# First batch of a windowed attention: casting loads on 128 rows, 64x64 matmuls per head, a new opening order

## The chip, the cores and the metric

The kernel runs on one core of a Trainium2 chip. The metric is device time in microseconds. The kernel before takes 319.98 us (median of 3 runs, 319.39 to 320.38).

## The reference

Attention with a symmetric window of 32, then a two-layer product with a leaky ReLU:

```python
# q, k, v: [8 batches, 8 heads, 576 tokens, 64]
scores = q @ k.T / 8, masked to |i - j| <= 32
attn   = softmax(scores)              # exp, row sums, division
x      = (attn @ v), heads side by side      # [4608, 512]
out    = leaky_relu(x @ w_in, 0.01) @ w_out  # w_in 512x2048, w_out 2048x512
```

## The kernel before

All matmuls run on bf16. Heads are taken in pairs: two heads of 64 columns fill 128 partitions. A batch has four pairs (`NPAIR`), and a batch's 576 tokens are worked in two halves of 288 (`HALF`), so that one attention step `i` is a batch, a half and a pair; batch 0 has steps 0 to 7, with half 0 in steps 0 to 3.

A step goes through four engines. `score(i)` multiplies keys and queries in five matmuls, one for each block of 64 keys that the window touches; ScalarE takes the exponential of both sets of 288 columns at once (`e`), and GpSimd multiplies it by the window's mask (`prob`, L282). `sums(i)` adds up the weights with a matmul by `ones_bd`, which is 1 in two diagonal blocks, and VectorE takes the reciprocal (L309). `product(i)` multiplies the weights with the values in five matmuls, and `scaled(i)` (L334) multiplies that by the reciprocal into `xT`, whose slice for pair `p` is the p-th of four chunks that `x @ w_in` sums over. To keep the two heads apart in matmuls over 128 rows, keys and values are stored as block diagonals, `kbd` and `vbd`, of 128x128 blocks with zeros off the diagonal; there are two buffers of each, which alternate by batch. They are cleared once, and only the diagonal blocks are written after that.

Queries and keys reach the kernel in one of two ways. In batches 0 and 1 (`b < BY_DMA`) they are loaded as 32-bit numbers on 96 rows (`load_qk`, L79), cast on VectorE or GpSimd (`cast_qk`, L197), transposed on TensorE (`transposes`, L225) and copied out of PSUM by ScalarE (L233, L239), after which `place_keys` copies the keys into `kbd` (L258). From batch 2 on, a transposing DMA does it. Values are loaded in two halves of 64 rows (`load_v`, L91) and cast into `vbd` (`cast_v`, L203 and L205). All these loads are issued by the SP queue. The weights `w_in` and `w_out` are cast by their DMAs, which GpSimd issues (L448, L452), in four quarters each.

The second part takes half by half (`g` = 0 to 15): 16 tiles `f` of hidden columns, each with four matmuls of 288 columns (`h_mms`, L348) and a leaky ReLU on ScalarE (`h_out`, L355), and for each 128 tokens one output tile of 16 matmuls (`o_tile`, L390).

The order of instructions is written out by hand (`manual_schedule`): an engine takes its instructions in the order in which the code records them and waits at each for its operands. The opening, from `cast_qk(0, 0, ...)` to the first tiles of half 1, is a list of such calls, with `keep_busy` matmuls between them that compute nothing of use; steps 4 to 7 are recorded between tiles of half 0 (`second_half`). From half 1 on, a plan of tiles with due times (`plan`, `due`, `spend`) records the attention steps of later batches between the tiles.

Of the kernel before, what the change touches and what calls it, by code (L numbers as in the profile page):

```python
# [9 lines left out]
FP32 = mybir.dt.float32  # L10
# [6 lines left out]
def kernel(  # L17
# [49 lines left out]

    def load_qk(b, p, behind=None):

        for into, src, name in ((qf, q, "qf"), (kf, k, "kf")):
            t = fload.tile([96, 2, RUN * D], FP32, name=f"{name}{p}")
# [13 lines left out]
    def load_v(b, p):  # L87

        t = fload.tile([128, NB, D], FP32, name=f"vf{p}")
        for a in range(2):  # L90
            nc.sync.dma_start(  # L91
                out=t[64 * a:64 * a + 64],
                in_=v[b, 2 * p + a].rearrange("(c p) d -> p c d", p=64),
            )
        vf[b, p] = t

    load_qk(0, 0)
    load_qk(0, 1)
    load_v(0, 0)
    load_qk(0, 2)  # L100
    load_qk(0, 3)
    for p in range(1, NPAIR):
        load_v(0, p)


    ident_f = const.tile([128, 128], FP32)
    make_identity(nc, ident_f)
    ident = const.tile([128, 128], BF16)
    nc.vector.tensor_copy(out=ident, in_=ident_f)

    ones_bd = const.tile([128, 128], BF16)
    nc.vector.memset(ones_bd, 0.0)
    nc.vector.memset(ones_bd[0:64, 0:64], 1.0)
    nc.vector.memset(ones_bd[64:128, 64:128], 1.0)


    qb = const.tile([96, NPAIR, RUN, 2, D], BF16)
    kb = const.tile([96, NPAIR, RUN, 2, D], BF16)

# [3 lines left out]
    nc.vector.memset(zero, 0.0)  # L123

    def clear(t, p):
        flat = t[:, p].rearrange("p n j -> p (n j)")
        nc.scalar.activation(
            out=flat, in_=zero.to_broadcast([128, NB * 128]), func=AF.Copy,
        )

    mask = [const.tile([128, 2, 2, EVEN], BF16, name=f"mask{i}") for i in range(2)]
    nc.vector.memset(mask[0][:, 1, :, 0:16], 0.0)
    nc.vector.memset(mask[1][:, 1, :, 128:EVEN], 0.0)
    nc.vector.memset(kbd[0], 0.0)
    clear(vbd[0], 0)
    clear(vbd[0], 1)
    clear(vbd[0], 2)


# [6 lines left out]
    win = const.tile([128, 2, 3, 64], BF16)  # L146
    nc.gpsimd.memset(win, 1.0)
    for lo in (0, 64):
# [3 lines left out]
            base=0, channel_multiplier=-1, pattern=[[1, 2], [0, 3], [2, 64]],  # L152
# [179 lines left out]
    def scaled(i):  # L332
        _, x, r = probs.pop(i)
        nc.vector.tensor_mul(place(i), x, r)  # L334
# [312 lines left out]
```

## Time and profile before

| | us |
|---|---|
| median of 3 runs | 319.98 (319.39 to 320.38) |
| span of the profiled execution | 318.5 |
| median less span | 1.5 |
| PE busy | 303.2 (95%) |
| VectorE (DVE) busy | 218.2 (69%) |
| GpSimd (POOL) busy | 191.6 (60%) |
| ScalarE (ACT) busy | 182.6 (57%) |
| PE busy, 0 to 5 us | 0.00 |
| PE busy, 5 to 10 us | 2.56 |
| PE busy, 10 to 15 us | 3.40 |
| PE busy, 20 to 25 us | 3.91 |

A profiled execution shows the span from the first to the last instruction; the measured time holds a little more. Busy time of an engine is the time in which one of its instructions runs; PEld is the loading of weights into the array, which runs beside the matmuls. Idle time costs something only where it lies on the chain of work that ends last. DMA queue q1 holds what SP issues and q0 what GpSimd issues; all of it runs on the same 16 DMA engines.

### The profile page before, as it was taken

The page shows a single profiled execution, that of the slowest core. Times are in us where ns is not written, and L with a number is a line of the kernel's source. Part 1 is how long each engine was busy: PE and PEld are TensorE (multiplying, and loading weights), DVE is VectorE, ACT ScalarE, POOL GpSimd, SP SyncE. Part 2 cuts the span into 40 slices and gives each one's busy share as a digit, 9 for nine tenths or more (in the row PEclk, how much of TensorE's full clock was granted, in tenths as well). Part 3 has the DMA queues.
Part 4 walks back from the last instruction along what each step waited for, and adds up shares of the span by engine and source line. Part 5 has one row for each costly group of instructions (what it writes and reads, how often), then busy time and mean ns, then how long its engine had stood idle before and what let it go on. Part 6 is the DMA issues. An engine that isn't in the chain of part 4 may idle for free.

```text
span 318.5 us, 6474 instructions
## 1 busy us (share of the span) xinstructions
PE 303.2 (95%) x2449; PEld 204.3 (64%) x2449; DVE 218.2 (69%) x259; ACT 182.6 (57%) x393; POOL 191.6 (60%) x251
## 2 busy tenths in 40 slices
PE   2679998999999999999999999999999999999996
PEld 1467774585765858576765858576665858576653
DVE  5678955869655997688755997688745988565100
ACT  7577698474652828374652828375552837464531
POOL 7798963974546866686546866586637866330000
PEclk9999999999999999999999999999999999999999
DMA  8999999997999995399735995399733430000101
GB/s 179 211 186 218 267 250 203 250 206 181 216 242 196 231 206 150 82 251 203 155 76 127 238 227 136 75 223 232 162 76 104 109 70 33 35 35 2 66 31 71
DMA packets 108400, 49.46 MB, mean 155 GB/s; under 512 B 68816, under 2 KB 103888, under 8 KB 108368
## 3 DMA queue, kind: packets, MB, share of 16 engines
q1 hardware_dynamic: 104144, 44.84, 66.8%
q0 software_dynamic: 4224, 4.19, 8.0%
q8 instruction: 19, 0.31, 0.4%
q14 instruction: 13, 0.11, 0.1%
HBM read 36.70 MB, written 9.44 MB: 145 GB/s over the span
## 4 chain that ended last, share of the span: by engine, by line
PE 89%; DMA 3%; DVE 2%; SPq 1%; POOL 1%; ACT 1%; issue 1%; DVEq 0%; ACTq 0%
PE mm L348 39%; PE mm L390 38%; PE x L320 5%; PE ps L275 4%; DMA kf<-in_k_dram 3%; PE s L301 2%; DVE r L309 2%; SPq L79 1%; POOL w_in_bf L448 1%; DVE xT L334 1%; PE tp L225 1%; PE s L304 1%; ACT vbd L203 0%; SPq L91 0%; POOL prob L282 0%
## 5 line engine op out<-in xcount | busy, mean ns | idle before, releaser
L309 DVE RECIPROCAL r<-s 128x288 f32<-128x288 f32 x64 | 125.2, 1956 | 56.5 <-PE s L301 53.3
L282 POOL TENSOR_TENSOR prob<-e,mask 128x576 bf16<-128x576 bf16 x64 | 81.5, 1274 | 87.8 <-ACT e L280 41.1
L348 PE MATMUL mm<-xT,w_in_bf 128*128 128x288 bf16 x1024 | 134.0, 286 | 0.3
L390 PE MATMUL mm<-w_out_bf,gT 128*128 128x512 bf16 (+2 forms) x592 | 130.4, 373 | 0.2 <-DMA w_out_bf<-in_moe_w_out_dram 0.2
L355 ACT ACTIVATE gT<-mm 128x288 bf16<-128x288 f32 x256 | 101.4, 412 | 24.8 <-PE mm L348 8.5
L348 PEld LDWEIGHTS <-w_in_bf 128*128 128x128 bf16 x1024 | 98.4, 98 | 24.8 <-issue 0.6
L390 PEld LDWEIGHTS <-gT 128*128 128x128 bf16 x592 | 56.3, 98 | 59.6 <-issue 0.3
L395 ACT ACTIVATE o_sb<-mm 128x512 f32<-128x512 f32 (+2 forms) x37 | 21.7, 586 | 92.0 <-PE mm L390 92.0
L280 ACT ACTIVATE e<-ps 128x576 bf16<-128x576 f32 x64 | 41.4, 648 | 9.4 <-PE ps L275 9.2
L197 POOL CAST kb<-kf 96x384 bf16<-96x384 f32 (+1 forms) x56 | 35.5, 656 | 4.6 <-DMA kf<-in_k_dram 4.6
L205 POOL CAST vbd<-vf 64x576 bf16<-64x576 f32 x50 | 34.5, 689 | 1.8 <-DMA vf<-in_v_dram 0.4
L334 DVE TENSOR_TENSOR xT<-x,r 128x288 bf16<-128x288 f32 x64 | 29.3, 458 | 8.2 <-PE x L320 1.2
L260 DVE COPY kbd<-kT 64x576 bf16<-64x576 bf16 x48 | 32.3, 672 | 0.3
L275 PE MATMUL ps<-qT,kbd 128*128 128x128 bf16 (+2 forms) x320 | 26.5, 215 | 1.8 <-DVE kbd L258 1.2
L275 PEld LDWEIGHTS <-kbd 128*128 128x128 bf16 x320 | 21.0, 100 | 10.6 <-DVE kbd L258 1.5
L320 PE MATMUL x<-prob,vbd 128*128 128x128 bf16 (+2 forms) x320 | 26.0, 213 | 1.3 <-ACT vbd L203 0.7
L197 POOL CAST qb<-qf 96x384 bf16<-96x384 f32 x48 | 24.5, 538 | 0.0
L320 PEld LDWEIGHTS <-vbd 128*128 128x128 bf16 x320 | 20.6, 99 | 3.9 <-ACT vbd L203 1.8
L292 DVE TENSOR_TENSOR both<-prob 128x288 bf16<-128x288 bf16 x52 | 19.7, 380 | 0.9
L301 PE MATMUL s<-both,ones_bd 128*128 128x288 bf16 x52 | 14.9, 286 | 0.0
L258 DVE COPY kbd<-kT 64x576 bf16<-64x576 bf16 x16 | 7.1, 444 | 8.7 <-ACT kT L239 8.6
L225 PE MATMUL tp<-ident,qb 96*128 96x96 bf16 x48 | 4.4, 243 | 6.2 <-DVE qb L197 6.2
(43 smaller groups left out, 86.6 us busy)
## 6 DMA issues: line engine op xcount, KB each, us to landing
qf<-in_q_dram SPq DMA_DIRECT2D x32, 288.0 KB, 4.5
kf<-in_k_dram SPq DMA_DIRECT2D x32, 288.0 KB, 5.0
vf<-in_v_dram SPq DMA_DIRECT2D x64, 144.0 KB, 4.2
out_dram<-o_sb SPq DMA_DIRECT2D x35, 256.0 KB, 3.6
w_in_bf<-in_moe_w_in_dram POOLq DMA_DIRECT2D x4, 512.0 KB, 8.6
w_out_bf<-in_moe_w_out_dram POOLq DMA_DIRECT2D x4, 512.0 KB, 16.8
qT<-qb SPq DMA_TRANSPOSE x24, 4.1
kT<-kb SPq DMA_TRANSPOSE x24, 3.2
```

Source lines behind the costliest of these rows:

```text
L197: eng.tensor_copy(out=to, in_=tok)
L205: nc.gpsimd.tensor_copy(out=vbd[b % 2][r, p, :, r], in_=vf[b, p][r])
L260: nc.vector.tensor_copy(out=to.rearrange("p n (m c) -> p n c m", c=2), in_=kT[r].rearrange("p (c n m) -> p n c m", c=2, n=NB),)
L275: nc.tensor.matmul(ps_v[:, n_, :, i0:i0 + n], kbd[b % 2][:, p, blk], by_c[:, :, hf * EVEN + i0:hf * EVEN + i0 + n], start=True, stop=True,)
L280: nc.scalar.activation(out=e, in_=ps[:, P0:P0 + 2 * HALF], func=AF.Exp, scale=scale)
L282: nc.gpsimd.tensor_mul(pr.rearrange("p n c i -> p (n c i)"), e, mask[hf].rearrange("p n c i -> p (n c i)"),)
L309: nc.vector.reciprocal(r, s)
L320: nc.tensor.matmul(x_v[:, :, i0:i0 + n], vbd[b % 2][:, p, blk, :], pr[:, n_, :, i0:i0 + n], start=(blk == parts[0][1]), stop=(blk == parts ...
L334: nc.vector.tensor_mul(place(i), x, r)
L348: nc.tensor.matmul(h[:, 0:HALF], w_in_bf[:, c, ts(f, 128)], xT[:, c, ds(g * HALF % RING, HALF)], start=(c == 0), stop=(c == DMC - 1),)
L355: nc.scalar.activation(out=gT[:, f, ds(g * HALF % RING, HALF)].rearrange("p (i c) -> p i c", c=2), in_=h[:, 0:HALF].rearrange("p (c i) -> ...
L390: nc.tensor.matmul(o[:, lo:hi], gT[:, f, ds(128 * j % RING, 128)], w_out_bf[:, f, lo:hi], start=(f == 0), stop=(f == FFC - 1),)
```

## The change

For batch 0, queries and keys are loaded by eight casting DMAs that GpSimd issues first of all (`load_first`), straight to bf16 on 128 rows: row `64a + i` holds nine consecutive tokens of head `a` of the pair. The two halves of each pair's values go on two load queues, SP and ScalarE. TensorE transposes 64x64 blocks (18 for each pair and operand, where there were six of 96 columns), and ScalarE or VectorE copies the result out (`evict_first`). Scores and products of batch 0 take each head by itself, in 64x64 matmuls on the two diagonal quarters of the array (ten each for a step, where there were five), with keys and values as they are; batch 0 writes no block diagonals, and tokens stay in their order there. The mask of batch 0 is read from a tile `wide` in overlapping slices, and VectorE multiplies it in some steps.

For batch 1 the block diagonals are written whole, zeros included, by a multiplication with a column that is 1 for one head and 0 for the other (`own_block`). The clears of the buffers at the start go away; buffer 0 is cleared by GpSimd during half 1, where buffer 1's clears stood. The tiles of queries and keys loaded on 96 rows are one allocation, and a GpSimd memset holds the loads of batch 1 as before, at another place in the order.

The opening is another list: 14 `keep_busy` matmuls at the start, all eight steps of batch 0 among the chunks and tiles of half 0, masks for later batches after them. Half 0's tiles are opened and closed apart (`h_open`, `h_close`), so that a tile's matmuls stand ahead of the step that the engine would wait for.

```diff
+    def load_first(p, which):
+        src, to = ((q, q0b), (k, k0b))[which == "k"]
+        nc.gpsimd.dma_start(
+            out=to[:, p].rearrange("i c d -> i (c d)"),
+            in_=src[0, 2 * p:2 * p + 2].rearrange("a (i c) d -> (a i) (c d)", c=ROW),
+        )
...
-    load_qk(0, 0)
-    load_qk(0, 1)
-    load_v(0, 0)
...
+    for p in range(NPAIR):
+        load_v(0, p, (0,))
+        load_v(0, p, (1,), nc.scalar)
+    load_first(0, "k")
+    load_first(0, "q")
     ident_f = const.tile([128, 128], FP32)
     make_identity(nc, ident_f)
+    for p in range(1, NPAIR):
+        load_first(p, "k")
+        load_first(p, "q")
...
-    nc.vector.memset(kbd[0], 0.0)
-    clear(vbd[0], 0)
...
+    def transpose_first(p, which):
+        src = (q0b, k0b)[which == "k"]
+        tp = mmps.tile([128, ROW, 64], BF16, name="tp", tag="mm")
+        for c in range(ROW):
+            for a in range(2):
+                r = slice(64 * a, 64 * a + 64)
+                nc.tensor.transpose(tp[r, c], src[r, p, c], ident[r, r])
...
+    def own_block(eng, out, in_, a):
+        if eng is nc.scalar:
+            eng.activation(out=out, in_=in_, func=AF.Copy, scale=own[:, a:a + 1])
+        else:
+            eng.tensor_scalar_mul(out=out, in0=in_, scalar1=own[:, a:a + 1])
...
     def score(i):
+        if b == 0:
...
+                    for r in HEADS:
+                        nc.tensor.matmul(
+                            by_n[r, n_, lo:hi], kTs[p][r, 64 * blk:64 * blk + 64],
+                            qT[b][r, p, hf * HALF + lo:hf * HALF + hi], start=True, stop=True,
+                        )
...
     def product(i):
+        if b == 0:
+            for r in HEADS:
+                for n_, blk, i0, n in parts:
+                    lo, hi = 2 * i0, 2 * (i0 + n)
+                    nc.tensor.matmul(
+                        x[r, lo:hi], v0b[r, p, blk], flat[r, n_, lo:hi],
...
+    keep_busy(ps, 0, 14, True)
+    fill(V)
+    transpose_first(0, "k")
+    evict_first(0, "k", A)
+    transpose_first(0, "q")
+    evict_first(0, "q", V)
+    transpose_first(1, "k")
+    score(0)
+    evict_first(1, "k", V)
+    transpose_first(1, "q")
+    exps(0)
+    value_first(0, V)
+    load_w_in(0, 512)
+    spread(A, GAP + 32, 2)
+    spread(V, 0, 3)
+    transpose_first(2, "k")
+    evict_first(1, "q", A)
+    masked(0, V)
+    load_w_in(512, 1024)
+    sums(0)
...
+    h_open(6)
+    h_close(3)
+    sums(6)
+    h_close(5)
+    product(5)
+    inverse(6)
...
+    product(7)
+    h_close(15)
+    scaled(7)
+    make_mask(0, nc.gpsimd)
+    make_mask(1, nc.gpsimd)
```

## The prediction

> **What bounds the kernel now.** I read the engine shares first (PE busy 95% of a span of 318.5 us, so time is won only where PE waits), then the chain of waits in order of time, cut to the opening:
>
> ```profile
> 5.83 9.66 DMA kf<-in_k_dram
> ...
> 15.54 0.82 POOL kb L197
> 16.36 2.35 POOL w_in_bf L448 x3
> ...
> 18.73 1.30 POOL prob L282
> ...
> 20.07 0.42 PE s L304 x2
> ...
> 26.39 0.65 PE mm L348 x4
> ```
>
> The opening hangs on the last key load (landed at 15.5), its cast and the weight issues on POOL, then on the attention steps, until from 26.4 us PE links itself. Next the table by stage (PE, PEld, DVE, ACT, POOL busy of each 5 us):
>
> ```profile
> 5.00:10.00 5.00, 2.56 (x26) 1.93 (x27) 2.12 (x4) 2.83 (x5) 3.43 (x6) 1.00 1.19 216
> 15.00:20.00 5.00, 4.25 (x32) 3.17 (x31) 4.38 (x7) 3.73 (x7) 4.50 (x7) 1.00 1.26 170
> 30.00:35.00 5.00, 5.00 (x50) 3.99 (x48) 4.52 (x5) 3.33 (x9) 4.98 (x6) 1.00 1.15 267
> ```
>
> PE is idle for most of the first 10 us, about 0.7 us in 15 to 20, and nothing from 30 on; DVE is nearly full from 15. So two things order the opening: when the first softmax can start, and then DVE's reciprocals. The timeline dates them, DVE first, then PE:
>
> ```profile
> 16.21 0.46 DVE L334 TENSOR_TENSOR xT<-x,r 128x288 bf16<-128x288 f32 x1
> 16.58 1.95 DVE L309 RECIPROCAL r<-s 128x288 f32<-128x288 f32 x1
> ...
> 25.88 0.46 DVE L334 TENSOR_TENSOR xT<-x,r 128x288 bf16<-128x288 f32 x1
> ```
> ```profile
> 16.97 0.65 PE L275 MATMUL ps<-qT,kbd 128*128 128x96 bf16 x5
> ...
> 20.32 0.40 PE L275 MATMUL ps<-qT,kbd 128*128 128x96 bf16 x5
> ...
> 35.12 4.46 PE L348 MATMUL mm<-xT,w_in_bf 128*128 128x288 bf16 x32
> ```
>
> Three marks: the first scaled step (step 0) ends at 16.67, the fourth (step 3, half 0 complete) at 26.34, and half 1's w_in products start at 35.12. After that mark both kernels run the same PE list behind the same stalls, so I price the change as the shift of the third mark. The score rows show a second thing: five scores take 0.65 us at 16.97 and 0.40 at 20.32. The array ran at half rate until about 19 us, though the granted-clock column reads 1.00 throughout.
>
> **Leg 1a, start to step 0.** Removed: 8 loads of 288 KB on SP, the casts L197 (DVE 0.56 to 1.8 each, POOL about 1.0), kbd copies (L258, 8 of 0.44), clears of kbd and vbd (DVE 1.98, ACT 3.27, POOL 1.06). Added: 8 casting loads on POOL, two queues for the values, 64x64 transposes (144 where 48 of 96 columns were) and 64x64 scores and products (160 for 80).
> - Issue. A POOL issue of w_in (512 rows) takes 0.75 to 0.93 us. Nothing shows one of 128 rows; by rows it could be 0.3. I take 0.6, nearer the shown row since part of it must be fixed. POOL starts at 0.82; eight issues 4.8, identity 0.5, the window select at a third of the columns 1.2: `win` is ready at 7.3 (8.9 at 0.8 each).
> - Landing. w_in's first packet came 1.7 us after its issue began (16.31 to 18.02 in the packet records). There 1024-byte cast packets run at 200 per us, 0.08 us each on one of 16 engines, 256-byte packets of v at 700 per us (0.023); and where w_out and q/k shared the engines, their packets alternated one to one (105 to 101 per us). So eight rounds of one 1152-byte cast packet (0.09) and two of v: 8 x 0.14 = 1.1 us. k0 lands near 3.7, q0 4.4, k1 5.5, q1 6.1, k2 6.8.
> - PE and evictions. ACT is free at 0.8 + four issues of 0.65 + table load 1.28 = 4.7; k0's eviction (0.65, as L239) ends at 5.5; q0's on DVE, about 0.75 (twice L334's 288 PSUM columns less its fixed part), at 6.7; score 7.5; exp 0.65, 8.3. DVE meanwhile evicts k1 and casts v0 (0.6), then spreads the mask (0.4) behind `win`: 8.8; masks on DVE, 0.7 (twice L292's 0.38, less its fixed part): 9.5; sums 0.45, reciprocal 1.96, scaled 0.46: 12.5. Taken between the two issue prices, 12.7 against 16.67: **-4.0**.
>
> **Leg 1b, step 0 to step 3.** In the new DVE list this holds a v cast 0.6, four reciprocals at 1.88 start to start (7.5), two masks (1.4; before, POOL did all), three scaled (1.3): 10.8, with 0.3 of waits 11.1, so 23.8. Before it took 26.34 - 16.67 = 9.7. **+1.4**.
>
> **Leg 2, step 3 to half 1.** PE has then: 52 w_in products of 0.1225 (6.4), two pairs of sums (0.5), four products of ten 64x64 matmuls (0.5 each at 45 to 50 ns, 2.0): 8.9, plus 0.6 of waits for reciprocals behind the tiles: 9.5, against 8.7 before. **+0.8**.
>
> Sum -4.0 + 1.4 + 0.8 = -1.8; I give back 0.3 because batch 1's order has its own stalls (0.4 at 37.0, ACT gT): **-1.5**.
>
> **Costs put at nothing.** The clears move to POOL among half 1's tiles, eight of 1.05, as many as buffer 1's clears there now (L540, L564); batch 2 needs them only after 60 us. The four mask copies (0.43) precede the key casts of batch 1, where six clears (6.1 us) stood. `own_block` replaces copies one for one (DVE 0.44, at worst 0.67 as L260: 8 x 0.23 = 1.8 us where DVE is busy 2.0 to 2.7 of 5); on ACT 0.68 as L203. Batch 1's SP loads start some 10 us earlier, since the POOL memset that holds them now stands behind fewer steps; that brings transfers, not work, forward. What this collides with: three queues share the engines, so the last v pair (144 packets per engine and queue, 0.14 a round) lands near 20.5, not 18.9, and ACT's cast of it precedes exp(7); its cover is the DVE chain, which reaches step 3's product at 22. The last w_in quarter lands near 30 and is wanted at 30.5: one us late costs about one us.
>
> **The 64x64 price.** No row has such a matmul. Lower bound: 128-wide ones already start 28 ns apart at 64 columns and 55 at 128 with weight loads hidden, and two tiles side by side could halve that. Upper: weights not hidden, half of the 98 ns (L348) to 129 ns (L225) that a 128-column load takes, some 50 ns more per matmul. I take them as hidden (28 transposing, 45 multiplying), the row they are nearest to.
>
> A rule speaks against this. In the Trainium skill, "TensorEngine Tiling (Array Packing)", Restrictions, column tiling switches off fast weight load, and Key Properties says that a change of tiling mode drains the engine; no trace here has either. By it the sum would be that of rival A.
>
> **The clock.** Before, the array sped up about 19 us in, in the first 5 us stretch with PE busy over 4 (4.25, above). The change runs 14 warm-up matmuls (0.187 each while slow, 2.6 us) from about 1.5 us, then transposes, a stretch as dense, so I take full rate from 5 to 8 us. If it comes at 17 instead, the 100 PE operations before the first sums run at 53 to 107 ns and some 1.0 us of the gain goes. The Trainium skill, "TensorE: Matmul & The Clock Gate", Part 1, has the clock freed by a busy window of about 3.4 us: 2.6 us of warm-up and the first transposes would just fill one; the late speed-up before agrees with it.
>
> **Rivals.**
> - A, slower: each tile loads its weights for itself while only the other tile multiplies. Extra 50 ns on the 40 product matmuls of leg 2 (2.0), and between step 0 and step 3 on 30 more (1.5) and, halved by the alternating heads, on 54 transposes and 50 scores (2.6), of which DVE's chain covers about 3.1: -1.5 + 2.0 + 1.0 = +1.5, **321.5**; with no overlap at all about +6, 326. It decides from about 12 ns extra per matmul. For it: half as many columns, twice the switches between modes. Against: no weight load is exposed in the trace even at 28 ns. 0.27.
> - B, no change: the clock comes late, or issues cost 0.8 to 0.9 and a w_in quarter is late by a half: **319.5**. For it: the 8 us of POOL issues are in series with `win`. 0.18.
> - C, larger gain: issues near 0.3 and two tiles at once: about -2.4, **317.6**. 0.10.
> - D, slower by one place: the cast loads start late because POOL's first issue is slow or v crowds them; 2 us late takes the whole gain: **320.5**. 0.05.
>
> My forecast has 0.40. The measurement can tell about 0.3% (0.96 us) from nothing. Faster by more: 0.40 + 0.10 and a part of B, 0.52; slower: A and part of D, 0.29; the rest, 0.19, same. The profiled execution has a span of 318.5, and the median is 319.98, 1.5 us more that lie outside the span; 318.5 - 1.5 + 1.5 gives **318.5**. The range reaches from C to the cheaper part of A: 317.0 to 322.6; left out are A without overlap and a gain beyond C.
>
> **What would show it.** In the new profile: first cast packets landed by 4 us and step 0's scaled ended near 12.7; step 3 near 23.8; half 1's w_in products from 33.4; transposing matmuls 28 ns apart, products 45. Scores still slow after 10 us mean the clock; transposes 50 ns or more apart after the speed-up mean A; a wait of `h_mms` on w_in near 30 means the crowded queue. I am wrong if the third mark moved but the end did not.

## The result and the profile after

The changed kernel takes 322.09 us (median of 4 runs, 321.74 to 322.25); the kernel before, on the same chip, 319.82 (4 runs, 319.39 to 320.38). The ratio is 1.0074, with a 95% interval of 1.0058 to 1.009: slower by 2.27 us where 1.5 us faster was forecast. The profiled execution has a span of 320.3 us, against 318.5. Medians and ranges, here and below, hold every execution; the ratios leave out those that took over 1.5% more than the fastest of their kernel, one in e4 and one in e7.

The chain of waits, cut to the opening, in order of time (start, length, what):

```profile
4.19 7.97 DMA kb<-in_k_dram
...
12.20 0.69 PE tp L216 x12
...
36.11 5.00 DVE qb L249
...
41.16 0.68 PE tp L277 x12
```

Before, the chain ran through the last key load until 15.5, and from 26.4 on it was for the most part TensorE's own work. Now a key load ends at 12.16 (pair 2's), and a piece stands in it that was not there: 5.00 us of a cast on VectorE at 36 us. The table by stage (PE, PEld, DVE, ACT, POOL busy):

```profile
5.00:10.00 5.00, 1.38 (x36) 1.11 (x36) 0.76 (x1) 0.65 (x1) 4.17 (x10) 1.00 1.27 206
15.00:20.00 5.00, 3.96 (x87) 2.70 (x83) 4.38 (x6) 2.84 (x5) 3.98 (x5) 1.00 1.24 204
30.00:35.00 5.00, 5.00 (x48) 3.81 (x48) 4.17 (x4) 3.04 (x8) 3.82 (x4) 1.00 1.16 268
40.00:45.00 5.00, 3.85 (x48) 3.28 (x48) 3.59 (x5) 3.70 (x9) 3.19 (x3) 1.00 1.23 209
```

From 5 to 10 us PE is busy 1.38 us, less than the 2.56 before, with the 16 engines of the DMA at their fullest (1.27). From 40 to 45 us it loses 1.15 us, where it lost nothing before. The marks, on VectorE's and TensorE's timelines (start, busy time; in brackets the idle time before it and what ended it):

```profile
15.62 0.46 DVE L428 TENSOR_TENSOR xT<-x,r 128x288 bf16<-128x288 f32 x1
...
26.26 0.39 DVE L428 TENSOR_TENSOR xT<-x,r 128x288 bf16<-128x288 f32 x1
...
36.11 4.99 DVE L249 CAST qb<-qf 96x768 bf16<-96x768 f32 x1
```
```profile
5.96 0.69 PE L216 MATMUL tp<-ident,kb 64*64 64x64 bf16 x18 [1.59 <-DMA kb<-in_k_dram]
...
10.15 0.69 PE L216 MATMUL tp<-ident,kb 64*64 64x64 bf16 x18 [2.27 <-DMA kb<-in_k_dram]
10.65 0.64 PE L333 MATMUL ps<-qT,kT 64*64 64x96 bf16 x10
...
35.63 4.38 PE L442 MATMUL mm<-xT,w_in_bf 128*128 128x288 bf16 x32
41.16 0.43 PE L277 MATMUL tp<-ident,qb 96*128 96x96 bf16 x6 [1.15 <-DVE qb L249]
```

Step 0's scaled ends at 16.08, 0.6 us earlier than before (forecast 4.0); step 3's at 26.65, 0.3 later; half 1's w_in products start at 35.63, 0.5 later (forecast 1.5 earlier). Then the wait of 1.15 us on the query cast is added: 0.5 and 1.15 are the lag that stays. TensorE's rows also show why pair 1's keys (10.15) delay step 0, which doesn't need them: in TensorE's list step 0's score (10.65) stands behind their transposes, as step 0's sums stand behind those of pair 2's keys. Beside that cast, POOL runs the clears that the change moved there:

```profile
36.35 1.05 POOL L715 MEMSET kbd<- 128x1152 bf16 x1
37.34 3.05 POOL L715 MEMSET vbd<- 128x1152 bf16 x3
40.35 1.44 POOL L249 CAST kb<-kf 96x768 bf16<-96x768 f32 x1
```

From step 12 on, each of VectorE's reciprocals stands 1.67 us behind its twin in the kernel before, to the end. Most of the rest of the 2.27 us is a matter of which execution was profiled: time less span is 1.7 us in every run that has both, so that before's, with its span of 318.5 us, is by estimate 0.4 us longer than its median run.

### The profile page after: what moved, and what is told of

The parts are those of the page before. It is cut to its first block, busy times and chain, and to the rows that moved or that the text cites. A ratio compares the mean times of both kernels' runs of the same rounds, so it can differ in the third digit from the quotient of the medians.

```text
span 320.3 us, 6796 instructions
## 1 busy us (share of the span) xinstructions
PE 304.8 (95%) x2618; PEld 204.3 (64%) x2618; DVE 216.4 (68%) x259; ACT 174.4 (54%) x383; POOL 185.3 (58%) x249
## 4 chain that ended last, share of the span: by engine, by line
PE 89%; DVE 5%; DMA 2%; issue 1%; POOL 1%; ACT 1%; DVEq 0%; ACTq 0%; POOLq 0%
PE mm L500 38%; PE mm L442 38%; PE x L413 4%; PE ps L341 4%; DMA kb<-in_k_dram 2%; DVE r L391 2%; PE s L378 2%; DVE qb L249 2%; PE s L381 1%; PE tp L277 1%; PE x L406 1%; DVE xT L428 0%; POOL prob L359 0%; POOL qb L102 0%; POOL kb L102 0%
## 5 line engine op out<-in xcount | busy, mean ns | idle before, releaser
L359 POOL TENSOR_TENSOR prob<-e,mask 128x576 bf16<-128x576 bf16 x56 | 71.3, 1273 | 91.6 <-ACT e L351 45.0
L351 ACT ACTIVATE e<-ps 128x576 bf16<-128x576 f32 x64 | 41.5, 648 | 15.7 <-PE ps L333 8.1
L257 POOL CAST vbd<-vf 64x576 bf16<-64x576 f32 x48 | 33.1, 690 | 1.4
L249 POOL CAST kb<-kf 96x384 bf16<-96x384 f32 (+1 forms) x52 | 31.4, 626 | 2.3 <-DMA kf<-in_k_dram 2.3
L315 DVE COPY kbd<-kT 64x576 bf16<-64x576 bf16 x48 | 32.2, 671 | 0.3
L413 PE MATMUL x<-prob,vbd 128*128 128x96 bf16 (+1 forms) x280 | 22.5, 211 | 1.1 <-ACT vbd L228 1.0
L341 PEld LDWEIGHTS <-kbd 128*128 128x128 bf16 x280 | 18.1, 98 | 8.2
L341 PE MATMUL ps<-qT,kbd 128*128 128x96 bf16 (+1 forms) x280 | 22.5, 211 | 0.0
L413 PEld LDWEIGHTS <-vbd 128*128 128x128 bf16 x280 | 18.0, 98 | 3.2 <-ACT vbd L228 1.3
L359 POOL TENSOR_TENSOR prob<-e,wide 128x576 bf16<-128x576 bf16 x5 | 6.5, 1305 | 5.4 <-ACT e L351 5.4
L381 PE MATMUL s<-prob,ones_bd 128*128 128x288 bf16 x24 | 5.4, 310 | 2.6 <-DVE r L391 2.4
```

What stands on the lines that cost most here:

```text
L249: eng.tensor_copy(out=to, in_=tok)
L257: nc.gpsimd.tensor_copy(out=vbd[b % 2][r, p, :, r], in_=vf[b, p][r])
L315: nc.vector.tensor_copy(out=to.rearrange("p n (m c) -> p n c m", c=2), in_=kT[r].rearrange("p (c n m) -> p n c m", c=2, n=NB),)
L341: nc.tensor.matmul(ps_v[:, n_, :, i0:i0 + n], kbd[b % 2][:, p, blk], by_c[:, :, hf * EVEN + i0:hf * EVEN + i0 + n], start=True, stop=True,)
L351: nc.scalar.activation(out=e, in_=ps[:, P0:P0 + 2 * HALF], func=AF.Exp, scale=scale)
L359: eng.tensor_mul(pr.rearrange("p n c i -> p n (c i)"), e.rearrange("p (n t) -> p n t", n=2), allowed,)
```

## The experiments

Theory: two causes. The queries' and keys' casting loads land late because the values' loads crowd them, so that leg 1a gained 0.6 us and not 4.0; and POOL's clears hold VectorE's casts up at 36 us. Rivals: A of the prediction (64x64 weight loads lie open), TensorE's late clock, loads bound by POOL's issues, and a cast that is slow for another reason.

A kernel is read here by five numbers of its profile: the start of VectorE's reciprocal in steps 0 and 3, the start of half 1's w_in products, the reciprocal of step 9, and the stretch between the last two, which holds the late stall alone.

| kernel | step 0 | step 3 | half 1 | step 9 | half 1 to 9 | median us (range) | ratio to before |
|---|---|---|---|---|---|---|---|
| before | 13.45 | 23.83 | 35.12 | 54.59 | 19.47 | 319.82 (319.39-320.38) | 1 |
| changed | 13.56 | 21.84 | 35.63 | 56.26 | 20.63 | 322.09 (321.74-322.25) | 1.0074 [1.0058, 1.009] |
| e1 | 13.56 | 21.84 | 35.63 | 54.94 | 19.31 | 322.61 (322.31-322.76) | 1.0094 [1.0079, 1.011] |
| e2 | 12.02 | 29.04 | 45.23 | 64.53 | 19.30 | 330.12 (328.78-332.88) | 1.0342 [1.0304, 1.038] |
| e3 | 11.28 | 27.86 | 46.40 | 65.70 | 19.30 | 333.76 (332.57-334.03) | 1.0438 [1.0416, 1.0459] |
| e4 | 12.01 | 20.85 | 34.65 | 54.81 | 20.16 | 321.19 (319.8-324.64) | 1.005 [1.0025, 1.0075] |
| e5 | 12.90 | 21.18 | 34.97 | 54.28 | 19.31 | 320.87 (320.02-321.76) | 1.0041 [1.0026, 1.0057] |
| e6 | 12.60 | 20.88 | 35.31 | 54.62 | 19.31 | 320.49 (319.74-323.96) | 1.005 [1.0022, 1.0077] |
| e7 | 13.18 | 20.99 | 35.19 | 54.49 | 19.30 | 320.53 (319.32-324.12) | 1.0032 [1.0016, 1.0048] |
| e8 | 14.41 | 28.19 | 41.98 | 61.28 | 19.30 | 326.83 (326.49-327.38) | 1.0233 [1.0209, 1.0256] |
| e9 | 13.79 | 21.83 | 39.67 | 58.97 | 19.30 | 324.73 (323.78-324.79) | 1.0142 [1.0121, 1.0163] |
| e10 | 12.52 | 20.79 | 39.47 | 58.77 | 19.30 | 323.23 (321.19-324.77) | 1.0103 [1.0074, 1.0131] |
| e11 | 12.49 | 21.21 | 35.00 | 54.30 | 19.30 | 320.08 (318.51-320.55) | 1.0006 [0.9991, 1.0021] |
| e12 | 12.00 | 19.81 | 33.52 | 52.82 | 19.30 | 319.48 (318.64-320.65) | 0.9993 [0.9977, 1.0008] |
| e13 | 12.41 | 21.10 | 34.81 | 54.11 | 19.30 | 319.46 (318.8-320.65) | 0.9992 [0.9976, 1.0008] |
| e14 | 12.53 | 21.00 | 34.70 | 54.00 | 19.30 | 319.72 (319.01-320.11) | 0.9996 [0.9985, 1.0007] |
| e15 | 11.41 | 19.36 | 33.05 | 52.36 | 19.31 | 319.63 (318.46-320.07) | 0.9989 [0.9974, 1.0004] |

Kernels are compared by their ratios, since the median of the kernel before lay between 319.5 and 319.9 from one set of runs to the next. The marks are those of one execution each, and they spread. The changed kernel, e1, e5 and e9 have the same opening until 25 us, and their step 0 lies between 12.90 and 13.79, their step 3 between 21.18 and 21.84; e4 and e6, alike until half 1, differ there by 0.66. So a difference of less than about 0.9 us between two kernels' marks in the first 36 us says nothing by itself, and that half 1 came 0.5 later than before is not shown to be more than this. The stretch from half 1 to step 9 is steady: 19.30 or 19.31 wherever TensorE does not wait for the late casts.

**e1_clears.** The clears away from the query casts:

```diff
+    for p in range(NPAIR):
+        nc.gpsimd.memset(kbd[0][:, p], 0.0)
     cast_qk(1, 0, nc.vector)
...
-        if f < 12:
-            nc.gpsimd.memset((kbd if f < 8 else vbd)[0][:, f % 4], 0.0)
...
+        if 5 <= turn < 9:
+            nc.gpsimd.memset(vbd[0][:, turn - 5], 0.0)
```

> The changed kernel with POOL's clears taken away from the stretch in which VectorE casts batch 1's queries (36 us after the start): the four of kbd go ahead of POOL's first key cast of batch 1, the four of vbd behind the score of step 9. Theory (POOL's memsets hold VectorE's f32-to-bf16 casts up): the first of the two query casts at 36 us takes 0.6 to 1.2 us instead of 5.0, batch 1's first transposes start near 40.0 instead of 41.16 (then behind the w_in products, no longer behind the cast), and the time falls by 1.0 to 1.3 us, to about 320.9 us. Rival (the casts are slow for another reason, DMA writes into the same partitions or the loads themselves): the cast still takes 3 us or more and the time stays at 322. Step 0's scaled stays at 15.6 in both.

VectorE's, TensorE's and POOL's timelines:

```profile
36.12 1.14 DVE L249 CAST qb<-qf 96x768 bf16<-96x768 f32 x2
```
```profile
39.86 0.42 PE L277 MATMUL tp<-ident,qb 96*128 96x96 bf16 x6
```
```profile
55.01 3.05 POOL L762 MEMSET vbd<- 128x1152 bf16 x3
58.02 1.28 POOL L359 TENSOR_TENSOR prob<-e,mask 128x576 bf16<-128x576 bf16 x1
```

The two casts take 1.14 us instead of 6.08 and the transposes follow the w_in products at 39.86 without a wait; step 9 is 1.32 us earlier. So the cause of the late stall is shown; the rival forecast a cast of 3 us or more. The time did not fall, because the other four clears now stood ahead of a mask in POOL's queue (58.02): step 9's reciprocal is 0.35 us behind the kernel before, step 11's 4.05. The forecast of the time missed that.

**e2_v_held** and **e3_both.** The values of pairs 1 to 3 held back; e3 has e1's edit as well:

```diff
-    for p in range(NPAIR):
-        load_v(0, p, (0,))
-        load_v(0, p, (1,), nc.scalar)
+    load_v(0, 0)
...
     evict_first(1, "k", V)
+    for p in range(1, NPAIR):
+        vf[0, p] = fload.tile([128, NB, D], FP32, name=f"vf{p}")
+        nc.vector.memset(vf[0, p][0:1, 0, 0:1], 0.0)
+        nc.vector.memset(vf[0, p][64:65, 0, 0:1], 0.0)
+        load_v(0, p)
```

> The changed kernel with only the first pair of batch 0's values loaded at the start, on SP, and the other three pairs held on SP behind a small write of VectorE after the eviction of pair 1's keys. Theory (the value loads crowd out the cast loads of queries and keys in the first 9 us): pair 0's keys are transposed at 5.0 to 5.6 instead of 5.96, pair 1's keys at 7.5 to 8.5 instead of 10.15, step 0's scaled starts at 13 to 14 instead of 15.6, step 3's follows by as much less what VectorE's reciprocals keep, and the time falls by 1 to 2 us. Rival 1 (the cast loads are bound by their own issue and descriptors on POOL): pair 1's keys still come at 9.5 or later and nothing moves. Rival 2 (the start is not what decides; the later stretch is): step 0 moves by 2 us and the time stays within 0.5 us of 322, the gain going into the wait for w_in or into VectorE's chain. The late casts of batch 1's queries stay slow in all.

> Both edits together: POOL's clears away from VectorE's query casts, and the values of pairs 1 to 3 held. If the two causes are independent, the gains add: 2 to 3.3 us below the changed kernel, 318.8 to 320.0, at or a little below the kernel before. If the late stall hides what the start gains (the casts wait for a fixed time, the landing of batch 1's loads), it gives no more than the clears alone, about 320.9; if the start cannot be moved, the same.

```profile
23.37 0.75 PE L404 MATMUL x<-prob,v0b 64*64 64x96 bf16 x10 [7.43 <-DVE v0b L143]
```

The first half of the theory held: pair 1's keys are transposed at 7.68 instead of 10.15, step 0's reciprocal starts 1.5 us earlier. But the held values met w_in. From 15 to 25 us the packet records show some 150 packets of 256 bytes (values) and 150 of 1024 bytes (w_in) in each microsecond: here the packets went one for one, not byte for byte, so the small ones got a fifth of the bytes, pair 1's values came at 22.8, and TensorE stood for 7.43 us; by the clock record it was not at full rate before 37 us. e2 lost some 8 us, e3 (with e1's misplaced clears) some 12. None of the forecasts had it. In e2 the clears still stretch the first query cast (3.13 us), but half 1 is so late that the cast ends before TensorE wants it: 19.30 from half 1 to step 9.

**e4_v_one_queue.** All eight value loads on SP:

```diff
-        load_v(0, p, (0,))
-        load_v(0, p, (1,), nc.scalar)
+        load_v(0, p)
```

> The changed kernel with all eight value loads of batch 0 on SP's queue, none on ACT's, all still issued at once at the start. If the DMA engines share themselves out queue by queue, one value queue against the cast queue leaves the casts a half instead of a third: pair 1's keys are transposed at about 9 instead of 10.15 and step 0's scaled starts about 1 us earlier, worth up to 0.8 us of the time; the values of pair 0 land later, near 5 us, which nothing waits for. If only the sum of bytes counts, pair 1's keys stay near 10 and the time at 322. Against it: SP issues eight loads at 0.75 us, so the values are spread out over 6 us by their issue alone, which would also help the casts of pair 0.

```profile
39.72 0.43 PE L276 MATMUL tp<-ident,qb 96*128 96x96 bf16 x6 [0.69 <-DVE qb L248]
```

Pair 1's keys come at 8.26, step 0's reciprocal 1.55 us earlier. Over all runs these keys land between 9.4 and 10.3 us where the values go on two queues (the changed kernel, e1, e5, e8, e9), between 7.9 and 9.1 in the nine with one queue, and at 7.0 and 7.6 where they are held (e3, e2), so the crowding of the landing is shown. What it costs in time e4 doesn't show: half 1 is 1.0 earlier (0.3 in e6, with the same opening), and the ratio falls by 0.0024 (0.8 us) with intervals that overlap. The late casts still take 5.63 us for two.

**e5_clears_apart** and **e6_clears_v_one_queue.** e1 with vbd's clears behind `score(9)`; e6 adds e4's edit:

```diff
             score(9)
+            for p in range(NPAIR):
+                nc.gpsimd.memset(vbd[0][:, p], 0.0)
```

> The clears moved again: kbd's four ahead of batch 1's first key cast as in e1_clears, vbd's four behind the score of step 9, into POOL's gap from 50 to 55 us, where e1_clears had them inside step 11's queue (its reciprocal of step 9 stood 0.35 us behind the kernel before, that of step 11 4.05 us). Theory: the query casts are short as in e1_clears (1.1 us for two), steps 8 to 63 keep the 0.3 us that step 8 of e1_clears showed against the kernel before, and the time is 1.3 us below the changed kernel: 320.6 to 321.0. Rival: the rest of the schedule takes the 1.3 us back wherever the clears stand (the stretch behind half 1 is bound by loads or by VectorE), and the time is 322 again.

> e5_clears_apart with the value loads of batch 0 on SP's queue alone, as in e4_v_one_queue. In e4_v_one_queue step 7's reciprocal stood 1.0 us ahead of the changed kernel's (31.37 against 32.35) and 1.45 of it was left at the end, with the slow casts still there. Theory: without the slow casts the 1.0 us of step 7 goes through: half 1's w_in products start at 34.65, batch 1's first transposes at 38.9, and the time is 1.0 us below e5_clears_apart, 319.7, at the time of the kernel before. Rival: the stretch behind is bound by batch 1's loads, whose last keys land near 39 whatever the start does, and the time is e5_clears_apart's.

```profile
25.34 0.50 PE L405 MATMUL x<-prob,v0b 64*64 64x96 bf16 x10 [1.13 <-ACT v0b L142]
```

e5 keeps what e1 found: half 1 to step 9 is 19.31 us, and the ratio falls from 1.0074 to 1.0041, 1.1 us, with intervals that do not meet. e6 did not add e4's gain: with one queue the last values come behind w_in, step 3's product waits 1.13 us for their copy (the row above is e6's), and half 1 starts at 35.31. Four of e6's twelve executions took 322.3 to 324.0 us, the others 319.7 to 320.7; of the sixty of e11 to e15, where w_in comes later, none took more than 320.7.

**e7_fill_clock.** e6 with 22 more `keep_busy` products in the gaps up to 11 us:

```diff
     transpose_first(0, "k")
+    keep_busy(ps, 0, 8)
...
     transpose_first(0, "q")
+    keep_busy(ps, 0, 8)
...
     transpose_first(1, "q")
+    keep_busy(ps, 0, 6)
```

> e6_clears_v_one_queue with 22 more warm-up products on TensorE in the gaps that it waits in: 8 behind pair 0's key transposes, 8 behind its query transposes, 6 behind pair 1's. In e1_clears the profile has TensorE at full rate from 4.0 to 7.4 us (18 transposes in 0.47 us of busy time instead of 0.69) and again at half from 7.4 to 17.7, and in e4_v_one_queue full rate comes at 20.1. Theory (the clock falls back because of the gaps from 5 to 11 us): with the gaps filled full rate stays from 4 or 5 us on, the w_in products of 17 to 20 us run at 0.65 us for four instead of 1.17, and the time falls by 0.5 to 1.5 us below e6_clears_v_one_queue. Rival (the clock follows a schedule of its own, or VectorE's chain decides the stretch anyway): full rate comes at 16 us or later, or comes early and moves the time by less than 0.3 us. If the fillers stand in the way of the transposes, step 0 is up to 1 us later.

Full rate held from 6.5 us to the end, and the median did not move (320.49 to 320.53); the ratio fell by 0.0018, inside the intervals. The six last fillers delayed step 0, whose exponential waited for them until 11.24; but steps 1 to 3, 0.1 us behind e6, where full rate came at 16.98, speak for VectorE and the loads as what sets this stretch, not TensorE's rate. An effect of less than about 1 us these runs cannot exclude; that the clock is not the cause of the loss follows from e14 below.

**e8_double_64.** Each 64x64 transpose and score of batch 0 issued twice:

```diff
-                nc.tensor.transpose(tp[r, c], src[r, p, c], ident[r, r])
+                for _ in range(2):
+                    nc.tensor.transpose(tp[r, c], src[r, p, c], ident[r, r])
...
-                    for r in HEADS:
+                    for r in HEADS * 2:
```

> The changed kernel with every 64x64 transpose and every 64x64 score product of batch 0 issued twice into the same place: 144 transposes and 80 score products more, nothing else. Theory (a 64x64 operation of either head costs about 15 ns at full rate and 27 at half, two heads side by side, its weight load hidden): each group of 36 transposes takes 0.5 us more at half rate, each score 0.15 to 0.3 more, some 4 us of TensorE time in all of which most lies beside the loads and VectorE's reciprocals, and the time rises by 0.3 to 1.5 us. Rival (weight loads of 64x64 operations lie open, 50 ns each): 224 more operations cost 11 us of TensorE time, the scores' share of it (4 us) on the path of every step, and the time rises by 3 us or more.

```profile
16.25 0.50 PE L334 MATMUL ps<-qT,kT 64*64 64x128 bf16 x13 [1.56 <-issue]
...
22.17 0.57 PE L217 MATMUL tp<-ident,qb 64*64 64x64 bf16 x25 [1.41 <-issue]
...
31.09 0.67 PE L334 MATMUL ps<-qT,kT 64*64 64x64 bf16 x20
31.60 0.47 PE L407 MATMUL x<-prob,v0b 64*64 64x96 bf16 x10
```

The price is the theory's: at half rate 18 more transposes took 0.49 us (27 ns each), and at full rate twenty scores take 0.51 us from their start to the next group's, where ten took 0.26. The time rose by some 5 us all the same, and neither theory has it: in two places TensorE stopped in the middle of a group, 1.56 and 1.41 us, waiting for nothing that the profile shows, and step 0's products came behind the first, step 1's behind the second. In the packet records a 16 KB packet of the instruction queue starts 0.7 and 0.9 us ahead of the two; that it is the cause is not shown, since the changed kernel has two such packets and no such stop. The clock record has half rate from 16.9 to 20.3 and from 23.7 to 27.1 besides. So the time alone would have spoken for rival A; the rows speak against it.

**e9_scaled3_first** and **e10_v_w_in_later.** e5 with step 4's reciprocal behind step 3's scaled; e10 has the values on one queue and three w_in quarters later besides:

```diff
     h_chunk(2)
-    inverse(4)
     score(7)
...
     scaled(3)
+    inverse(4)
     inverse(5)
```
```diff
     masked(1, G)
+    load_w_in(512, 1024)
...
     masked(2, G)
+    load_w_in(1024, 1536)
+    load_w_in(1536, 2048)
```

> e5_clears_apart with one instruction of VectorE moved: step 4's reciprocal (1.95 us) stands behind step 3's scaled instead of ahead of it. In the changed kernel step 3's product is there at 25.5 and its scaled waits for the reciprocal until 26.26; the last quarter of the sum of w_in's first four tiles starts behind it. Theory (the stretch up to half 1 is set by VectorE's order until step 3's scaled, and by TensorE's own work from there): step 3's scaled starts 0.5 to 0.9 us earlier, half 1's w_in products as much, and the time falls by 0.5 to 0.8 us below e5_clears_apart, to about 320.2. Rival 1 (the reciprocals of steps 4 to 7 are the chain): they come later by 0.4 us, and half 1 starts at the same time or later. Rival 2 (the start's loads set it all): no change of more than 0.2 us.

> e9_scaled3_first with the values of batch 0 on SP's queue alone and the last three quarters of w_in issued later, one behind step 1's mask and two behind step 2's (they were issued from 8.7 to 12.3 us), so that neither the query and key casts nor the last values share the DMA engines with them. In e6_clears_v_one_queue the first reciprocal was 0.3 us ahead of e5_clears_apart's, but step 3's product waited 1.13 us for the copy of the last values, whose 256-byte packets went packet by packet with w_in's. Theory (the loads' order on the 16 engines decides the start): the last values are there by 20 us, no wait for them is left, steps 1 to 7 run 0.8 to 1.3 us ahead of e9_scaled3_first, and the time is 0.5 to 1.2 us less, about 319.2, a little below the kernel before. Rival: the w_in quarters come too late (wanted from 26 us on, landing 2.5 us apart from 20 on), TensorE waits for them in half 0, and the time is that of e9_scaled3_first or up to 2 us more.

TensorE's timeline of e9:

```profile
27.88 0.64 PE L381 MATMUL s<-prob,ones_bd 128*128 128x288 bf16 x2 [2.41 <-DVE r L391]
28.32 1.16 PE L442 MATMUL mm<-xT,w_in_bf 128*128 128x288 bf16 x4
```

Both lost some 3 us to the swap (e9 against e5; e10 against e11, which has e10's loads without the swap, and 16 fillers), by a way that the expectations lacked. Sums have one PSUM buffer, so step 5's sums wait for step 4's reciprocal, and on TensorE they stand ahead of the last w_in chunk that step 3's earlier scaled had freed. In e9 that wait of 2.41 us cost twice: from 26.7 to 33.5 us the clock record shows half rate, four w_in products take 1.16 us of busy time where they take 0.65, and half 1 starts at 39.67. In e10, which has the same wait of 2.41 us, the rate had already fallen at 22.8, so there the wait is not what brought it down. Against e9 it gained 0.0039 in ratio (1.2 us): the last values came in time, with no wait of step 3's product on them; it is the part that e11 keeps.

**e11_loads_and_fill** and **e12_less_on_dve.** e6 with w_in's quarters later and 6 and 10 fillers behind pair 0's transposes; e12 takes two instructions from VectorE:

```diff
+    value_first(1, G)
-    value_first(1, V)
...
-    masked(5, V)
+    masked(5, G)
```

> e6_clears_v_one_queue with the last three quarters of w_in issued later, as in e10_v_w_in_later (but with the reciprocal of step 4 back in its place), and with warm-up products in two gaps only: 6 behind pair 0's key transposes and 10 behind its query transposes, none ahead of step 0's exponential, which in e7_fill_clock waited for the last of them until 11.24. Theory (loads in the wrong order, a clock that falls back in the gaps, and the clears are the three losses): step 0's reciprocal at 12.0 to 12.6, no wait for the last values ahead of step 3's product (1.13 us in e6_clears_v_one_queue), half 1's w_in products at 34.0 to 34.5 instead of 35.31, and the time 0.8 to 1.3 us below e6_clears_v_one_queue, 319.2 to 319.7, beside the kernel before. Rival (VectorE's chain of eight reciprocals, 2.45 us a step, sets the stretch whatever the loads do): less than 0.4 us below e6_clears_v_one_queue. If w_in's later quarters are late, TensorE waits in half 0 and the time is 321 or more.

> e11_loads_and_fill with two instructions taken from VectorE between its reciprocals and given to POOL: the cast of pair 1's values (0.48 us) and step 5's mask (0.45 us, 1.27 on POOL). Theory (VectorE's chain sets steps 1 to 4): the reciprocals of steps 1 to 4 come 0.3 to 0.8 us earlier and the time falls by 0.3 to 0.7 us below e11_loads_and_fill, to about 319. Rival (TensorE's sums wait for the one sum buffer, which the reciprocal before them frees, so that a step takes 2.45 us with or without the rest): no change of more than 0.2 us.

VectorE's and TensorE's timelines of e12:

```profile
12.00 1.96 DVE L390 RECIPROCAL r<-s 128x288 f32<-128x288 f32 x1 [0.71 <-PE s L380]
```
```profile
33.52 4.38 PE L441 MATMUL mm<-xT,w_in_bf 128*128 128x288 bf16 x32
```

e11 is level with the kernel before (1.0006), e12 as well (0.9993): 0.8%, 2.6 us, below the changed kernel. Between e5 and e11, whose intervals do not meet, stand the one value queue, w_in's later quarters and the fillers; e14, below, has no fillers and is level too, so the order of the loads brings back what e5 still lost. e11's half 1 (35.00) missed its forecast of 34.0 to 34.5. In e12's profile steps 0 and 9 and half 1 are 1.5 to 1.8 us ahead of before's, step 3's reciprocal 4.0; that execution, 318.91, lies 0.6 us under its median. The difference between e11 and e12 is inside their intervals.

**e13_sums0_first** and **e14_no_fill.** e12 with step 0's sums and step 1's score ahead of pair 2's key transposes; e14 without the fillers:

```diff
-    value_first(0, V)
...
-    transpose_first(2, "k")
     evict_first(1, "q", A)
     masked(0, V)
+    value_first(0, V)
     sums(0)
-    evict_first(2, "k", A)
     score(1)
+    transpose_first(2, "k")
+    exps(1)
+    evict_first(2, "k", A)
```

> e12_less_on_dve with TensorE's order changed at the start: step 0's sums and step 1's score stand ahead of the transposes of pair 2's keys, on whose landing they waited (transposes at 11.14, sums at 11.54, while step 0's mask ends near 11.2), step 1's exponential ahead of the copy of those keys, and VectorE's cast of pair 0's values behind step 0's mask instead of ahead of it. Theory (what is left of the late step 0 is that its sums wait in TensorE's queue for a load they don't need): step 0's reciprocal starts at 11.3 to 11.6 instead of 12.0, step 1's at 14.0 to 14.5 instead of 14.87, and the time is 0.3 to 0.7 us below e12_less_on_dve, 318.8 to 319.2, under the kernel before. Rival (VectorE's chain of reciprocals and the landing of w_in's first quarter at 17.6 take it back): steps 3 to 7 and the time as in e12_less_on_dve within 0.2 us.

> e13_sums0_first without the 16 warm-up products in the gaps of the first 9 us (the 14 at the start stay). Theory (the gaps let TensorE's clock fall back): full rate comes at 16 us or later as in the changed kernel, or falls back in between; the groups of the start run at half rate (a score 0.64 us of busy time instead of 0.43), the first two sets of w_in products at 1.17 us instead of 0.66 in some executions, and the time is 0.3 to 1.5 us more than e13_sums0_first, with a wider spread of runs. Rival (loads and VectorE decide the start, the clock does not): within 0.3 us of e13_sums0_first.

No change: 0.9992 and 0.9996. Step 0's reciprocal was not even earlier (12.41), because its mask now waited for ScalarE's copy of the window until 11.46. The fillers are worth no more than the runs can tell. e14's profiled execution ran at half rate from 8.9 to 15.7 us and is level with the kernel before all the same, so a late clock is not the cause of the changed kernel's 2.27 us.

**e15_more_fill.** 12 more fillers between 10 and 17 us in e12:

```diff
+    keep_busy(ps, 0, 6)
     transpose_first(2, "k")
...
     product(1)
+    keep_busy(ps, 0, 3)
...
     score(3)
+    keep_busy(ps, 0, 3)
```

> e12_less_on_dve with 12 more warm-up products: 6 ahead of the transposes of pair 2's keys, 3 behind step 1's products, 3 behind step 3's score, where TensorE waits anyway. In e12_less_on_dve's profile full rate held from 5.9 us to the end (step 9's reciprocal 1.77 us ahead of the kernel before, 318.91 us), in that of e11_loads_and_fill and e13_sums0_first it fell back to half from 17.4 to 21 us (0.28 and 0.48 ahead, 320.31 and 320.17). Theory (what spreads the runs from 318.6 to 320.7 is whether the clock falls back between 14 and 21 us): with those gaps filled it seldom does, most runs come at 318.6 to 319.2, the median falls by 0.4 to 0.8 us below e12_less_on_dve's, under the kernel before by 0.2%. Rival (the fall-back does not follow these gaps, or the fillers delay step 1 to 3 by what they bring): median and spread as before, 319.3 to 319.8.

Its profile is the best of all (span 316.7, full rate from 5.6 us on), its median is not: 319.63, spread from 318.46 to 320.07, ratio 0.9989. Ten of its twelve executions have a granted clock of 0.998 or more and still spread from 318.46 to 319.86; what makes that spread stays open. No version is faster than the kernel before by more than the runs can tell.

## Why the prediction was wrong

Two steps failed: the landing of the loads in leg 1a (0.6 us gained and not 4.0) and the clears among the costs put at nothing (1.15 us of wait). With legs 1b and 2 as measured the changed kernel's profile reads -0.6 + 0.9 + 0.2 + 1.15 = +1.65, about the lag from step 12 on.

**Leg 1a, landing: the term that failed.** It was sized at 1.1 us a load with overlapping, from one cast packet for two of v: k0 at 3.7, k1 at 5.5, k2 at 6.8. TensorE got k0 at 5.96, k1 at 10.15, k2 at 12.20. Three parts of it are measured. POOL's first load was issued at 1.31, not 0.82 (the issue price, 0.54 to 0.73 against 0.6, was right). A cast packet took 106 ns in the median and not 90, so that a load of 128 packets costs the 16 engines 0.9 us even in e2, where the values of one pair alone were beside it; the forecast had the four loads behind k0 follow within 3.1 us (3.7 to 6.8), less than four times that. In e2 k1 landed at 7.6 and k2 at 9.6, so about half of the delay (2.5 of 4.6 us for k1) is the crowding and the rest is not. And the share was no fixed one to two: from 6 to 8 us the packet records hold 51 cast packets against 1514 of v, in e4 210 against 759. This is rival D's mechanism, which had 0.05. Step 0's exponential, which follows the score behind k1's transposes, ended at 11.99 and not at 8.3, 3.7 us later; from there to the end of its scaled the chain took 4.1 us (4.2 forecast). So the whole of the start's lag of 3.4 us behind the forecast lies ahead of that score.

**Leg 1a, the clock.** Full rate was taken from 5 to 8 us; it came at 16.87. In e1's execution the warm-up did free the clock, and it fell back; TensorE's rows of e1:

```profile
5.72 0.47 PE L216 MATMUL tp<-ident,kb 64*64 64x64 bf16 x18 [1.37 <-DMA kb<-in_k_dram]
...
10.15 0.69 PE L216 MATMUL tp<-ident,kb 64*64 64x64 bf16 x18 [2.22 <-DMA kb<-in_k_dram]
```

The same 18 transposes show 0.47 us at 5.72 and 0.69 at 10.15; the clock record has full rate from 4.2 to 7.6 and half from there to 17.9. The Trainium skill, "TensorE: Matmul & The Clock Gate", Part 1, has free-running windows of 3413 ns that free the clock when busy and close it again when idle. The records agree in length: 3.41, 6.83 and 10.24 us long, one, two and three such windows. They do not agree on idle: in the first 40 us of these runs full rate ended after windows in which TensorE was busy for 0 to 65% of the time (51% in e9, from 23.28 to 26.69), and it stayed after others with 59 to 63%. The prediction drew only the first half of that rule: that the 14 products would free the clock, not that the wait behind them would take it back. The price put on it, 1.0 us, was not confirmed: between e6 and e7 and between e13 and e14 the difference is inside the intervals, and e15, at full rate from 5.6 us, took 5.4 us from the start of step 0's score to the end of its scaled, as long as the changed kernel at half rate.

**Legs 1b and 2** were about right in this one profile: 10.6 us from step 0 to step 3 (11.1 forecast, 9.7 before), 9.0 from step 3 to half 1 (9.5 forecast, 8.8 before). They cost 0.9 and 0.2 where 1.4 and 0.8 were set aside, and with a start only 0.6 us earlier that still left half 1 0.5 us later.

**Costs put at nothing: the clears.** Eight of them on POOL were covered by "as many as buffer 1's clears there now". They were as many, but not in the same place: six of buffer 1's eight are recorded among half 0's tiles (L540) and were over at 37.97, only two among half 1's (L564), where all eight of buffer 0's stand now. Four of these ran from 36.35 to 40.4, behind a key cast that waited for its load, and so beside the first query cast, on which batch 1's first transposes wait; the 0.3 us given back for stalls of batch 1's order did not cover the 1.15. e1 and e5 show the price, 1.3 us from half 1 to step 9, and the cause. The row was there to see, in the kernel before, on VectorE's and POOL's timelines:

```profile
36.54 2.93 DVE L197 CAST qb<-qf 96x768 bf16<-96x768 f32 x2
...
42.15 0.56 DVE L197 CAST qb<-qf 96x768 bf16<-96x768 f32 x1
```
```profile
35.92 2.05 POOL L540 MEMSET vbd<- 128x1152 bf16 x2
37.93 2.23 POOL L197 CAST kb<-kf 96x768 bf16<-96x768 f32 x2
```

The first of the two casts at 36.54 took 1.84 us beside the memsets, the second 1.16 beside a cast of POOL, and the one at 42.15 took 0.56 with no memset beside it; the prediction quoted "0.56 to 1.8" without asking what made it 1.8. The stretch follows the memsets: the first query cast takes 1.84 us in the kernel before, 2.59 in e8, 3.13 in e2, 4.54 in e4 and 4.99 in the changed kernel, and ends 0.4 to 0.7 us after the last memset beside it each time; in the twelve kernels that have none there it takes 0.55 to 1.19. The Trainium skill, "SBUF — State Buffer", SBUF: two separate sides, has VectorE (in its two-port modes) and GpSimd share one port pair, which goes to the one that starts first for its whole instruction, while the other is blocked. The trace agrees in kind and is harsher: the cast started at 36.11, beside a POOL cast and 0.24 us ahead of the first memset, stood through four memsets in a row, 4.99 us, and ended 0.7 us after the last. Such a wait shows as busy time of the blocked engine, not as idle time.

The marks also settle "I am wrong if the third mark moved but the end did not": in this profile the third mark moved the wrong way by 0.5 us, and the end by 1.2 us more than the mark.

**Rival A and the 64x64 price.** The range held the time, and A's 321.5 was the nearest number, by luck and for no reason of A's. Ten products take 0.42 us at full rate (42 ns each, 45 taken), ten scores 0.26, 18 transposes 0.33 (18 ns, 28 taken): no weight load lies open in these rows of the changed kernel:

```profile
16.79 0.49 PE L216 MATMUL tp<-ident,qb 64*64 64x64 bf16 x18
17.12 0.48 PE L406 MATMUL x<-prob,v0b 64*64 64x96 bf16 x10
...
29.52 0.48 PE L406 MATMUL x<-prob,v0b 64*64 64x64 bf16 x10
29.94 2.13 PE L442 MATMUL mm<-xT,w_in_bf 128*128 128x288 bf16 x16
```

The price is read from one group's start to the next's. The rule that spoke against the change, column tiling without fast weight load (the Trainium skill, "TensorEngine Tiling (Array Packing)", Restrictions), shows no cost in these rows.

**The other covers** held: w_in's last quarter landed at 27.0 (30 forecast), the last values at 14.4 (20.5 forecast), since from 6 to 8 us nearly all packets were the values'. That early landing and the late keys go together; why the casts had so few packets then is not shown. `own_block` took 0.50 on VectorE (0.44 to 0.67 forecast), the four mask copies 1.5 us in all.

The mended kernels' profiles lead before's by 0.3 to 2.2 us at step 9, while their ratios are level. Most of that is which execution was profiled: of e12's lead of 1.8 us, 0.6 is that its execution lies under its median and 0.4 (the estimate above) that before's lies over it; of e15's 2.2, 1.2 and 0.4. The granted clock goes with the rest of the spread in part. In each of e11 to e15 the executions with a granted clock under 0.998, 35 of 60, took 0.6 to 1.5 us more on average than the others of the same kernel, 0.7 over all five; of 118 executions of the kernel before one was under 0.998. No run shows that the fall of the clock is the cause of this, and a late start of full rate does not show in that figure.

What stays open: the part of the fallen clock in the mended kernels' times, why they gain nothing on the kernel before although step 0 starts up to 2.0 us earlier (e15), and the two stops of TensorE in e8.

## What to carry to other kernels

Before calling a moved instruction free, look at what it will run beside, not only at whether its engine has room: a memset on POOL stretched a VectorE cast from 0.6 to 5 us, with no idle time on VectorE to show for it, and an unexplained factor of three between two rows of the same instruction was the warning. When loads are spread over more queues, price each by its packets on the shared engines and ask which load is wanted first; issuing everything at once gave the early turns to the load that was wanted last. And where an instruction is moved ahead in one engine's list, follow the buffer it frees as well as the result it makes.

## What the runs showed of the hardware

- Where two queues had work, packets mostly went one for one and not byte for byte: 150 of 256 bytes and 150 of 1024 in each microsecond (e2, 15 to 25 us), so that the load in small packets got a fifth of the bytes. It is not always so: from 6 to 8 us in the changed kernel 51 cast packets went against 1514 of the values.
- VectorE's cast from 32 to 16 bits (96x768): 0.55 us alone, 1.17 beside a POOL cast, 1.84 (kernel before) and 4.99 (changed kernel) beside POOL memsets. VectorE's 16-bit multiplication into kbd took 0.51 with a memset beside the first 0.33 of it (42.86 us, changed kernel), 0.50 without.
- In e9 half rate set in within a wait of 2.4 us on TensorE and cost 1.9 us more (the sixteen w_in products behind it take 1.09 and 2.86 us to the next group's start, in the changed kernel 0.58 and 1.48).
- In e8, with 224 more instructions on TensorE at the start, it stopped twice, for 1.56 and 1.41 us, and the profile names no releaser.
